# Attention in groups of two tiles in a windowed attention + SoLU MoE kernel, with PSUM shared out anew and the sync queue reordered

## The chip, the cores and the metric

The kernel runs on one core of one Trainium2 chip. The metric is the device time of one execution in microseconds (us). The engines are named as in the profile: PE (TensorE) does matrix multiplies into PSUM, PEld is its weight load, DVE is VectorE, ACT is ScalarE, POOL is GpSimd, and SP is the sync engine, whose queue (SPq) issues every DMA of this kernel.

## What is computed

Attention with a causal window of 64 keys, in 8 heads of 64, then one SoLU feed-forward layer on the joined heads. The reference, cut to what matters:

```python
scores = scale * np.matmul(q, k.transpose(0, 1, 3, 2))          # (8, 8, 576, 576), D = 64
mask = (rel >= 0) & (rel < 64)
scores = np.where(mask, scores, -1e9); scores -= np.max(scores, axis=-1, keepdims=True)
attn = np.exp(scores); attn = attn / (np.sum(attn, axis=-1, keepdims=True) + 1e-09)
x = np.matmul(attn, v)                                          # heads joined: (4608, 512)
h = x @ w_in                                                    # (4608, 1024)
e = np.exp(h - np.max(h, axis=-1, keepdims=True))
solu = h * (e / (np.sum(e, axis=-1, keepdims=True) + 1e-09))
ln = (solu - mean(solu)) / np.sqrt(var(solu) + 1e-06) * g_ln
out = ln @ w_out                                                # (4608, 512)
```

All inputs and the output are fp32.

## The kernel before

The 4608 tokens are cut into 36 tiles of 128. Each tile t goes through these steps (line numbers are those of the kernel before):

- `load(t)` (L336, L340): two DMAs on SP, qk (640 KB) and v (512 KB).
- `scores(t)` on PE (L364): 32 small matmuls, 64x64 weights against 64x128, into `pS`. Below they are called S.
- `softmax(t)`: eight masked row maxima on DVE (L379, out of `pS` into `sS`), eight exponentials on ACT (L384), a reciprocal of the sums on DVE (L397, L400) and eight scalings on POOL (L402), one per head.
- `cross(t)`: the scaled weights have to be transposed. From tile 5 on ACT splits them into two planes of 16 bits (L416, two copies into a `raw` buffer), two DMA transposes on SP turn the planes round (L419), and `transposes(t)` puts them together on DVE (L426, two copies into `PT`). Tiles 0 to 4 are transposed on PE (L439).
- `values(t)` on PE (L463): 32 small matmuls of 128x64 weights into `pX`, called V below. ACT rounds the result into `xH` (L477), and DVE takes the rest into `xL` (L478).
- `moe_in(t, h)` on PE (L506): two halves of 12 matmuls of 128x128 against 128x512 into `pH`, which holds two banks and has one buffer. Each fp32 product is made of three passes, xH by the high weights, xH by the low ones, xL by the high ones. All 24 are called I.
- `moe_norm(t)`: row maximum on DVE (L521), exponential on ACT (L523), product and sum on DVE (L526), then sums, a square on ACT (L532), a power on POOL (L539), and two scalings on POOL (L543, the halves of `e`). After L526 `pH` is free for the next tile.
- `moe_cross(t)` and `moe_transpose(t)`: the halves of `e` go the same way, DVE copy (L569), DMA transpose (L572), DVE copy (L582), ACT cast to `yH` (L586), DVE remainder `yL` (L588). The first three and the last two tiles are transposed on PE (L605).
- `moe_out(t)` on PE (L642): 24 matmuls like those of I into `pO`, called O. ACT copies the result (L649), and a DMA on SP stores it (L650).

A main loop over t (L682) records these steps as a plan: in iteration t it records `load(t+4)`, I(t), the norm of t, V(t+1), S(t+3) with its softmax and cross, and O(t-2). PE and SP keep the order of recording (`edges`, L71), unless an operation is marked loose. Every other engine's order is made by a list scheduler (`order`, L109): each operation carries a cost written in the code, its due time comes from PE's order, and whatever is due first among the ready operations goes next. The result is written out as one fixed sequence for each engine, and each engine runs its own in order. Buffers are rings (`RINGS`, L46): a tile of a ring waits for the last reader of the one that held its place before.

PSUM has eight banks here: `pH` two, `pS` two (one buffer), `t` two (transposes on PE, one bank each), `pX` one, `pO` one.

Of the kernel before, what the change touches and what calls it, by code (L numbers as in the profile page):

```python
# [18 lines left out]
P = 128  # L19
# [7 lines left out]
AHEAD = 3  # L27
# [13 lines left out]
CROSS_P = 5  # L41

# [121 lines left out]
def tile_window_attention_solu_moe(  # L164
# [156 lines left out]
    def QK(t):  # L321
        return T("qk", t, [P, NPAIR * (2 * P + WIN)])
# [10 lines left out]
    def load(t, parts=range(2)):  # L333

        if 0 in parts:
            plan.dma(P * P * 40, lambda: nc.sync.dma_start(QK(t), qk[t]), [], [("qk", t)])  # L336


        if 1 in parts:
            plan.dma(P * P * 32, lambda: nc.sync.dma_start(  # L340
                T("v", t, [P, 2, DM]).rearrange("p a n -> p (a n)"), v[t]), [], [("v", t)])

# [69 lines left out]
    def cross(t):  # L412
        if t < CROSS_P:
            return
        for x in range(2):
            plan.op("ACT", 1050, lambda x=x: nc.scalar.copy(  # L416
                XP(t)[:, x], SS(t)[:, 4 * x:4 * x + 4].bitcast(U16).rearrange("p h (n w) -> p w (h n)", w=2)),
                [("sS", t, 4 * x + i) for i in range(4)], [("raw", NW + 2 * t, x)])
            plan.op("SP", 1250, lambda x=x: nc.sync.dma_start_transpose(  # L419
                XP(t)[:, 2 + x].rearrange("p w (h n) -> p (w h) n", h=4), XP(t)[:, x].rearrange("p w n -> p (w n)")),  # L420
                [("raw", NW + 2 * t, x)], [("raw", NW + 2 * t, 2 + x)], 2600)

    def transposes(t):
        if t >= CROSS_P:
            for x in range(2):
                plan.op("DVE", 740, lambda x=x: nc.vector.tensor_copy(  # L426
                    PT(t)[:, 4 * x:4 * x + 4].bitcast(U16).rearrange("p h (n w) -> p h w n", w=2),
                    XP(t)[:, 2 + x].rearrange("p w (h n) -> p h w n", h=4)),
                    [("raw", NW + 2 * t, 2 + x)], [("PT", t, x)])
            return  # L430
        for x in range(2):
            n = 4 * t + x

            def pA(n=n):
                return T("t", n, [P, 4, P], pool=ps_t)
# [5 lines left out]
            plan.op("PE", 430, emit, [("sS", t, 4 * x + i) for i in range(4)], [("t", n)], loose=t < LOOSE)  # L441
            plan.op(
                "DVE" if x and t >= EARLY else "ACT", 600, lambda x=x, pA=pA:
                (nc.vector.tensor_copy if x and t >= EARLY else nc.scalar.copy)(PT(t)[:, 4 * x:4 * x + 4], pA()),  # L444
                [("t", n)], [("PT", t, x)])

    def PX(t):
        return T("pX", t, [P, NC, P], pool=ps_x)

# [6 lines left out]
    def values(t):  # L456
# [11 lines left out]
        if t < PLAIN_IN:  # L468
            for x in range(2):
                ps = slice(2 * x, 2 * x + 2)  # L470
                plan.op("PE", 550, lambda x=x: emit((2 * x, 2 * x + 1)), [("PT", t, x)] + vals, [("pX", t, x)],
                        loose=t < LOOSE)
                plan.op("ACT", 360, lambda ps=ps: nc.scalar.copy(XH(t)[:, ps], PX(t)[:, ps]),
                        [("pX", t, x)], [("xH", t, x)])
            return
        plan.op("PE", 1100, emit, [("PT", t, x) for x in range(2)] + vals, [("pX", t)])
        plan.op("ACT", 560, lambda: nc.scalar.copy(XH(t), PX(t)), [("pX", t)], [("xH", t)])  # L477
        plan.op("DVE", 620, lambda: nc.vector.tensor_sub(XL(t), PX(t), XH(t).bitcast(F32)),  # L478
                [("pX", t), ("xH", t)], [("xL", t)])

# [84 lines left out]
    def moe_cross(t):  # L565
        if not crosses(t):
            return
        for h in range(2):
# [23 lines left out]
    def moe_transpose(t):  # L592
# [3 lines left out]
        for h in range(2):  # L596
            n = 4 * t + 2 + h

            def pT(n=n):
                return T("t", n, [P, 4, P], pool=ps_t)  # L600

# [5 lines left out]
            hs = slice(4 * h, 4 * h + 4)  # L607
            plan.op("PE", 430, emit, [("e", t, h)], [("t", n)])
            if t < PLAIN_OUT:
                plan.op("DVE", 620, lambda hs=hs, pT=pT: nc.vector.tensor_tensor(  # L610
                    YH(t)[:, hs], pT(), g_sb[:, hs].unsqueeze(2).to_broadcast([P, 4, P]), op=ALU.mult),
                    [("t", n), ("g",)], [("yH", t, h)])
                continue
            plan.op("ACT", 560, lambda hs=hs, pT=pT: nc.scalar.copy(YH(t)[:, hs], pT()),
                    [("t", n)], [("yH", t, h)])
            plan.op("DVE", 620, lambda hs=hs, pT=pT: nc.vector.tensor_sub(
                YL(t)[:, hs], pT(), YH(t)[:, hs].bitcast(F32)),
                [("t", n), ("yH", t, h)], [("yL", t, h)])

    def moe_out(t, middle=None):  # L620

        other = t >= NTILE - BEHIND and (NTILE - t) % 2 == 0
        tag = ("pX", NTILE + t) if other else ("pO", t)

        def PO():
            return T(*tag, [P, DM], pool=ps_x if other else ps_o)

# [22 lines left out]
        plan.dma(P * DM * 4, lambda: nc.sync.dma_start(out[t * P:(t + 1) * P, :], ot()), [("ot", t)], [])  # L650

# [109 lines left out]
```

## Time and profile before

| | |
|---|---|
| median of 3 runs | 532.76 us (531.51 to 532.77) |
| profiled execution, its own time | 533.39 us |
| its span, first to last instruction | 531.6 us |
| PE busy | 511.5 us (96%) |
| DVE, ACT, POOL busy | 415.4, 352.4, 213.9 us |
| mean granted PE clock | 0.996 |
| data moved by DMA | 93.56 MB |

The span leaves 1.8 us of the profiled execution's own time outside. A row of the timeline reads: start in us from the span's start, duration in us, engine, line, operation, output <- inputs, count, and in square brackets the idle time of the engine before it. A row of the groups reads: line, engine, operation, names, shapes, count | busy us, mean ns of one | idle us just before them. A row of the windows reads: stretch, its length, then busy us and count for PE, PEld, DVE, ACT, POOL, then the granted PE clock as a share of full speed, DMA share and GB/s. An fp32 matmul of V or S is one instruction of the program and two records in the profile (x16 in the program's order is x32 in the timeline).

### The profile page before, as it was taken

What the parts mean: (1) busy time and instruction counts of PE and PEld (TensorE: products, weight loads), DVE (VectorE), ACT (ScalarE), POOL (GpSimd) and SP (SyncE); (2) the same over time, 40 slices, a digit from 0 to 9 for tenths busy, and PEclk for the clock granted to TensorE, in tenths of its full rate; (3) what the DMA queues carried; (4) which work ended last, traced back from release to release, by engine and by line L of the source; (5) the groups of instructions that cost most, each with busy time, mean ns of one, the idle gap of its engine ahead of it and who ended that gap; (6) DMA issues with size and microseconds to landing.
All of it is one profiled execution on the core that took longest, in us unless ns stands there. A gap on an engine that the chain in (4) does not pass through costs nothing.

```text
span 531.6 us, 11607 instructions
## 1 busy us (share of the span) xinstructions
PE 511.5 (96%) x4072; PEld 393.2 (74%) x4072; DVE 415.4 (78%) x1327; ACT 352.4 (66%) x959; POOL 213.9 (40%) x406
## 2 busy tenths in 40 slices
PE   2789999999999999999999999999999999999997
PEld 1345566777777887777777777777777777777785
DVE  4969998878888888888887888888878888887630
ACT  4479866677777777777777776666666666676331
POOL 2036077344443444444443444444444444444130
PEclk9999999999999999999999999999999999999999
DMA  8992107687788778777888877777778777774411
GB/s 318 408 357 110 65 2 179 171 182 187 186 189 187 191 189 188 190 188 179 187 173 166 207 182 186 181 187 184 176 171 197 189 184 184 183 182 75 100 41 39
DMA packets 148506, 93.56 MB, mean 176 GB/s; under 512 B 132960, under 2 KB 132960, under 8 KB 148064
## 3 DMA queue, kind: packets, MB, share of 16 engines
q1 hardware_dynamic: 148448, 92.83, 68.3%
q8 instruction: 32, 0.52, 0.4%
q14 instruction: 26, 0.21, 0.1%
HBM read 50.86 MB, written 9.44 MB: 113 GB/s over the span
## 4 chain that ended last, share of the span: by engine, by line
PE 94%; ACT 2%; DVE 2%; DMA 1%; POOL 0%; issue 0%; ACTq 0%; DVEq 0%
PE pO L642 36%; PE pH L506 34%; PE pX L463 7%; PE pS L364 7%; PE pH L495 4%; PE pO L630 3%; PE pX L642 1%; DMA qk<-qk 1%; PE t L605 1%; ACT sS L384 1%; PE t L439 1%; ACT w L285 0%; POOL e L543 0%; DVE mst L521 0%; ACT e L523 0%; ACT PT L444 0%
## 5 line engine op out<-in xcount | busy, mean ns | idle before, releaser
L402 POOL TENSOR_SCALAR sS<-sS,rec 128x128 f32<-128x128 f32 x280 | 116.9, 439 | 49.8 <-DVE nmx L379 27.0
L384 ACT ACTIVATE sS<-sS,nmx 128x128 f32<-128x128 f32 x288 | 112.6, 395 | 9.7 <-DVE nmx L379 9.4
L539 POOL TENSOR_TENSOR mst<-mst,neghalf 128x1 f32<-128x1 f32 x36 | 20.6, 571 | 235.1 <-DVE mst L537 235.1
L642 PE MATMUL pO<-w_outH,yH 128*128 128x512 f32 x264 | 108.1, 410 | 0.0
L506 PE MATMUL pH<-w_inH,xH 128*128 128x512 f32 x264 | 105.8, 401 | 0.0
L642 PE MATMUL pO<-w,yH 128*128 128x512 f32 x264 | 104.6, 396 | 0.0
L506 PE MATMUL pH<-w,xH 128*128 128x512 f32 x264 | 104.2, 399 | 0.0
L642 PE MATMUL pO<-w_outH,yL 128*128 128x512 f32 x264 | 103.7, 393 | 0.0
L506 PE MATMUL pH<-w_inH,xL 128*128 128x512 f32 x264 | 103.6, 392 | 0.0
L477 ACT CAST xH<-pX 128x512 fp32r<-128x512 f32 x33 | 19.4, 587 | 112.6 <-PE pX L463 112.6
L543 POOL TENSOR_SCALAR e<-e,mst 128x512 f32<-128x512 f32 x72 | 73.5, 1028 | 18.4 <-DVE rec L397 11.0
L416 ACT COPY raw<-sS 128x1024 uint16<-128x1024 uint16 x62 | 62.2, 1051 | 6.2 <-POOL sS L402 6.1
L521 DVE TENSOR_REDUCE mst<-pH 128x1 f32<-128x1024 f32 x36 | 44.0, 1224 | 26.0 <-PE pH L506 25.2
L569 DVE COPY raw<-e 128x1024 uint16<-128x1024 uint16 x62 | 46.6, 752 | 21.9 <-POOL e L543 21.9
L642 PEld LDWEIGHTS pO<-w_outH,yH 128*128 128x128 f32 x264 | 49.5, 187 | 16.0 <-issue 5.0
L506 PEld LDWEIGHTS pH<-w_inH,xH 128*128 128x128 f32 x264 | 49.5, 188 | 13.5 <-issue 0.5
L506 PEld LDWEIGHTS pH<-w_inH,xL 128*128 128x128 f32 x264 | 49.6, 188 | 12.6 <-DVE w L310 0.2
L642 PEld LDWEIGHTS pO<-w_outH,yL 128*128 128x128 f32 x264 | 49.6, 188 | 12.3
L506 PEld LDWEIGHTS pH<-w,xH 128*128 128x128 f32 x264 | 49.6, 188 | 11.6 <-issue 0.2
L642 PEld LDWEIGHTS pO<-w,yH 128*128 128x128 f32 x264 | 49.6, 188 | 10.2
L384 ACT ACTIVATION_READ_ACCUMULATOR sS<-sS,nmx 128x1 f32 x288 | 55.2, 192 | 0.0
L379 DVE CUSTOM_DVE_ANT_0 sS<-pS,maskNone 128x128 f32<-128x128 f32 x224 | 51.1, 281 | 4.0 <-PE pS L364 3.9
(73 smaller groups left out, 777.5 us busy)
## 6 DMA issues: line engine op xcount, KB each, us to landing
qk<-qk SPq DMA_DIRECT2D x36, 640.0 KB, 4.8
v<-vS SPq DMA_DIRECT2D x36, 512.0 KB, 5.5
y<-ot SPq DMA_DIRECT2D x36, 256.0 KB, 2.6
raw<-w_out SPq DMA_DIRECT2D x4, 1024.0 KB, 10.1
raw<-w_in SPq DMA_DIRECT2D x3, 1024.0 KB, 11.5
raw<-raw SPq DMA_TRANSPOSE x124, 3.2
raw<-w_in SPq DMA_DIRECT2D x2, 512.0 KB, 6.5
g_sb<-gT SPq DMA_DIRECT2D x1, 4.0 KB, 14.9
```

The costliest lines, as they stand in the source:

```text
L364: nc.tensor.matmul(PS(t)[half * WIN:(half + 1) * WIN, r, p], q[rs, p, half * WIN:(half + 1) * WIN], keys, start=True, stop=True)
L379: plan.op("DVE", 215, lambda h=h: nc.vector.tensor_tensor_reduce(SS(t)[:, h], PS(t)[:, h % 2, h // 2], mk, scale=-SCALE, scalar=BIG, op0=A ...
L384: plan.op("ACT", 390, lambda h=h: nc.scalar.activation(SS(t)[:, h], SS(t)[:, h], AF.Exp, bias=cols("nmx", h), scale=-1.0, accum_out=cols(" ...
L402: plan.op(engine, cost, lambda h=h: v.tensor_scalar(SS(t)[:, h], SS(t)[:, h], rec()[:, h:h + 1], 0.0, ALU.mult, ALU.add), [R], [("sS", t, h)])
L416: plan.op("ACT", 1050, lambda x=x: nc.scalar.copy(XP(t)[:, x], SS(t)[:, 4 * x:4 * x + 4].bitcast(U16).rearrange("p h (n w) -> p w (h n)", ...
L463: nc.tensor.matmul(PX(t)[r * D:(r + 1) * D, p, ks], V(t, half)[:, h * D:(h + 1) * D], PT(t)[:, h, ks], start=True, stop=True)
L495: plan.op("PE", 860, lambda c=c, x=x: nc.tensor.matmul(PH(t)[:, x * 512:(x + 1) * 512], XH(t)[:, c], W32(c)[:, x], start=(c == 0), stop=(c ...
L506: plan.op("PE", 233, lambda n=n, c=c, x=x, w=w: nc.tensor.matmul(PH(t)[:, hs], x(t)[:, c], WH(c, h) if w is WH else WL(c)[:, h], start=(n ...
L521: plan.op("DVE", 1150, lambda: nc.vector.tensor_reduce(nmax(), PH(t), axis=AX.X, op=ALU.max, negate=True), [("pH", t)], [key(0)])
L543: plan.op("POOL", 770, lambda h=h, hs=hs: nc.gpsimd.tensor_scalar(E(t)[:, hs], E(t)[:, hs], nmean(), kk(), ALU.add, ALU.mult), [key(4), ke ...
L569: plan.op("DVE", 740, lambda h=h: nc.vector.tensor_copy(EP(t, h), E(t)[:, h * 512:(h + 1) * 512].bitcast(U16).rearrange("p (n w) -> p w n" ...
L642: plan.op("PE", 233, lambda f=f, i=i, x=x, k=k, y=y, w=w: nc.tensor.matmul(PO(), y(t)[:, f], w(i, x), start=(f == k == 0), stop=(f == NF - ...
```

## The change

**Groups of two.** Until iteration 6 the loop is as before, except that in iteration 6 scores of two tiles (9 and 10) follow V(7). Iteration 7 has V(8) alone. From iteration 8 on each even iteration records V(t+1), V(t+2), S(t+3), S(t+4) one behind the other on PE between I(t) and O(t-2), and each odd one records neither. `transposes` of both tiles are recorded at the even iteration. The count of every instruction of the steps stays what it was.

**PSUM.** `pS` gets a second buffer of two banks. The transposes on PE no longer have banks of their own (`t` is gone) and use buffers of `pS`. `pX` is gone, too: V writes into the ring `pO`, which now has two banks and holds V's and O's results in turn. So in a group the ring is taken by V(t+1), V(t+2), O(t-2), O(t-1), and O(t-2) waits until `xH` and `xL` of tile t+1 have been taken out of its bank.

**The sync queue.** DMAs of tiles after the third (loads, transposes, stores) are marked loose: SP no longer keeps them in the order of recording, the scheduler places them by due time. Loads of qk and v are recorded apart.

The core of the diff:

```diff
+PAIRS = 6
+SPL = 3
...
-    "pS": 1, "pH": 1, "t": 2, "pX": 1, "pO": 1,
+    "pS": 2, "pH": 1, "pO": 2,
...
-    def dma(self, size, emit, reads, writes):
-        self.op("SP", max(350, size // 340), emit, reads, writes, 2600)
+    def dma(self, size, emit, reads, writes, loose=False):
+        self.op("SP", max(350, size // 340), emit, reads, writes, 2600, loose)
...
-            plan.dma(P * P * 40, lambda: nc.sync.dma_start(QK(t), qk[t]), [], [("qk", t)])
+            plan.dma(P * P * 40, lambda: nc.sync.dma_start(QK(t), qk[t]), [], [("qk", t)],
+                     t > SPL)
...
+    def PP(t, x):
+        return PS(2 * NTILE + t)[:, x]
+    def PE_T(t, x):
+        return PS(NTILE + t)[:, x]
...
     def PX(t):
-        return T("pX", t, [P, NC, P], pool=ps_x)
+        return T("pO", NTILE + t, [P, NC, P], pool=ps_o)
...
+    def group(t):
+        on(values, t + 1)
+        if t != PAIRS:
+            on(values, t + 2)
+        both = t + AHEAD, t + AHEAD + 1
+        for u in both:
+            on(scores, u)
+        for u in (t + AHEAD + 2, t + AHEAD + 3):
+            on(load, u, range(1))
+        for u in (t + AHEAD + 1, t + AHEAD + 2):
+            if u != PAIRS + AHEAD + 2:
+                on(load, u, range(1, 2))
+        for u in both:
+            on(softmax, u)
+            on(cross, u)
+
     for t in range(NTILE + BEHIND):
-        on(load, t + AHEAD + 1)
+        if t < PAIRS:
+            on(load, t + AHEAD + 1)
+        if t == PAIRS - 1:
+            on(load, t + AHEAD + 2, range(1))
...
-            on(transposes, t + 1)
+            even = (t - PAIRS) % 2 == 0
+            if t <= PAIRS + 1:
+                on(transposes, t + 1)
+            elif even:
+                on(transposes, t + 1)
+                on(transposes, t + 2)
...
-            on(values, t + 1)
-            attend(t)
+            if t < PAIRS:
+                on(values, t + 1)
+                attend(t)
+            elif t == PAIRS + 1:
+                on(values, t + 1)
+                on(load, t + AHEAD + 1, range(1, 2))
+            elif even:
+                group(t)
```

**Where instructions move.** On PE, in the middle of the program, the order of before between I(16) and O(14), and between I(17) and O(15). In the names the first number is the buffer's own count, which is the tile (in the ring `pO` of the changed kernel V's tiles count on from 36, so `pO_53` is V of tile 17), the second a running number.

```order
L506 MATMUL pH_16_2863<-w_inH_103,xL_16_2802 128x512
L463 MATMUL pX_17_2915<-PT_17_2870,v_17_2556 64x64 x16
L364 MATMUL pS_19_2938<-qk_19_2859 64x128 x16
L642 MATMUL pO_14_2963<-w_outH_104,yH_14_2842 128x512
...
L506 MATMUL pH_17_3026<-w_inH_103,xL_17_2965 128x512
L463 MATMUL pX_18_3078<-PT_18_3033,v_18_2719 64x64 x16
L364 MATMUL pS_20_3101<-qk_20_3022 64x128 x16
L642 MATMUL pO_15_3126<-w_outH_104,yH_15_3005 128x512
```

The same place on PE in the changed kernel:

```order
L513 MATMUL pH_16_2868<-w_inH_97,xL_16_2687 128x512
L470 MATMUL pO_53_2915<-PT_17_2871,v_17_2387 64x64 x16
L470 MATMUL pO_54_2935<-PT_18_2897,v_18_2631 64x64 x16
L373 MATMUL pS_19_2959<-qk_19_2402 64x128 x16
L373 MATMUL pS_20_2986<-qk_20_2707 64x128 x16
L646 MATMUL pO_14_3009<-w_outH_98,yH_14_2866 128x512
...
L513 MATMUL pH_17_3072<-w_inH_97,xL_17_2968 128x512
L646 MATMUL pO_15_3139<-w_outH_98,yH_15_3092 128x512
```

V(18) and S(20) have moved ahead by one O and one I, and I(17) now goes straight over into O(15).

On ACT, the exponential of `moe_norm` of tile 15 (L523, later L530) and what stands around it. Before:

```order
L649 COPY ot_12_2709<-pO_12_2637 128x512
L532 ACTIVATE sq_14_2713,mst_14_2607<-e_14_2634,mst_14_2607 128x1024
L384 ACTIVATE sS_17_2647,sm_17_2668<-sS_17_2647,nmx_17_2648 128x128 x3
L477 CAST xH_16_2784<-pX_16_2752 128x512
L523 ACTIVATE e_15_2797,mst_15_2770<-pH_15_2700,mst_15_2770 128x1024
L416 COPY raw_42_2813<-sS_17_2647 128x1024 x2
L384 ACTIVATE sS_18_2810,sm_18_2831<-sS_18_2810,nmx_18_2811 128x128 x2
```

The same place on ACT in the changed kernel (`raw_42` and `raw_44` are the planes of tiles 17 and 18):

```order
L393 ACTIVATE sS_18_2719,sm_18_2766<-sS_18_2719,nmx_18_2720 128x128 x8
L653 COPY ot_12_2803<-pO_12_2680 128x512
L425 COPY raw_42_2810<-sS_17_2694 128x1024 x2
L530 ACTIVATE e_15_2836,mst_15_2817<-pH_15_2749,mst_15_2817 128x1024
L425 COPY raw_44_2849<-sS_18_2719 128x1024 x2
L593 CAST yH_14_2866<-y_14_2845 128x512
L653 COPY ot_13_2875<-pO_13_2813 128x512
```

The exponentials of tile 18 and the two plane copies of tile 17, which wait for POOL's scalings of that tile, now stand ahead of the exponential of tile 15; before, the copies stood behind it.

More of the change, by code (lines that the diff above doesn't have):

```diff
@@ L420, in cross @@
                 XP(t)[:, 2 + x].rearrange("p w (h n) -> p (w h) n", h=4), XP(t)[:, x].rearrange("p w n -> p (w n)")),
-                [("raw", NW + 2 * t, x)], [("raw", NW + 2 * t, 2 + x)], 2600)
+                [("raw", NW + 2 * t, x)], [("raw", NW + 2 * t, 2 + x)], 2600, t > SPL)
     def transposes(t):
@@ L431, in transposes, with pA @@
         for x in range(2):
-            n = 4 * t + x
-            def pA(n=n):
-                return T("t", n, [P, 4, P], pool=ps_t)
+            def pA(x=x):
+                return PP(t, x)
             def emit(x=x, pA=pA):
@@ L439, in emit @@
                     nc.tensor.transpose(pA()[:, i], SS(t)[:, 4 * x + i], ident)
-            plan.op("PE", 430, emit, [("sS", t, 4 * x + i) for i in range(4)], [("t", n)], loose=t < LOOSE)
+            plan.op("PE", 430, emit, [("sS", t, 4 * x + i) for i in range(4)], [("pS", 2 * NTILE + t, x)], loose=t < LOOSE)
             plan.op(
@@ L470, in values @@
                 ps = slice(2 * x, 2 * x + 2)
-                plan.op("PE", 550, lambda x=x: emit((2 * x, 2 * x + 1)), [("PT", t, x)] + vals, [("pX", t, x)],
+                plan.op("PE", 550, lambda x=x: emit((2 * x, 2 * x + 1)), [("PT", t, x)] + vals, [("pO", NTILE + t, x)],
                         loose=t < LOOSE)
                 plan.op("ACT", 360, lambda ps=ps: nc.scalar.copy(XH(t)[:, ps], PX(t)[:, ps]),
-                        [("pX", t, x)], [("xH", t, x)])
+                        [("pO", NTILE + t, x)], [("xH", t, x)])
             return
-        plan.op("PE", 1100, emit, [("PT", t, x) for x in range(2)] + vals, [("pX", t)])
-        plan.op("ACT", 560, lambda: nc.scalar.copy(XH(t), PX(t)), [("pX", t)], [("xH", t)])
+        plan.op("PE", 1100, emit, [("PT", t, x) for x in range(2)] + vals, [("pO", NTILE + t)])
+        plan.op("ACT", 560, lambda: nc.scalar.copy(XH(t), PX(t)), [("pO", NTILE + t)], [("xH", t)])
         plan.op("DVE", 620, lambda: nc.vector.tensor_sub(XL(t), PX(t), XH(t).bitcast(F32)),
-                [("pX", t), ("xH", t)], [("xL", t)])
+                [("pO", NTILE + t), ("xH", t)], [("xL", t)])
     def PH(t):
@@ L573, in moe_cross @@
                 TP(t, h).rearrange("p w f n -> p (w f) n"), EP(t, h).rearrange("p w n -> p (w n)")),
-                [("raw", NW + 2 * t + 1, h)], [("raw", NW + 2 * t + 1, 2 + h)], 2600)
+                [("raw", NW + 2 * t + 1, h)], [("raw", NW + 2 * t + 1, 2 + h)], 2600, t > SPL)
     def moe_join(t):
@@ L596, in moe_transpose, with pT @@
         for h in range(2):
-            n = 4 * t + 2 + h
-            def pT(n=n):
-                return T("t", n, [P, 4, P], pool=ps_t)
+            def pT(h=h):
+                return PE_T(t, h)
             def emit(h=h, pT=pT):
@@ L607, in moe_transpose @@
             hs = slice(4 * h, 4 * h + 4)
-            plan.op("PE", 430, emit, [("e", t, h)], [("t", n)])
+            plan.op("PE", 430, emit, [("e", t, h)], [("pS", NTILE + t, h)])
             if t < PLAIN_OUT:
@@ L611, in moe_transpose @@
                     YH(t)[:, hs], pT(), g_sb[:, hs].unsqueeze(2).to_broadcast([P, 4, P]), op=ALU.mult),
-                    [("t", n), ("g",)], [("yH", t, h)])
+                    [("pS", NTILE + t, h), ("g",)], [("yH", t, h)])
                 continue
             plan.op("ACT", 560, lambda hs=hs, pT=pT: nc.scalar.copy(YH(t)[:, hs], pT()),
-                    [("t", n)], [("yH", t, h)])
+                    [("pS", NTILE + t, h)], [("yH", t, h)])
             plan.op("DVE", 620, lambda hs=hs, pT=pT: nc.vector.tensor_sub(
                 YL(t)[:, hs], pT(), YH(t)[:, hs].bitcast(F32)),
-                [("t", n), ("yH", t, h)], [("yL", t, h)])
+                [("pS", NTILE + t, h), ("yH", t, h)], [("yL", t, h)])
     def moe_out(t, middle=None):
-        other = t >= NTILE - BEHIND and (NTILE - t) % 2 == 0
-        tag = ("pX", NTILE + t) if other else ("pO", t)
+        tag = ("pO", t)
         def PO():
-            return T(*tag, [P, DM], pool=ps_x if other else ps_o)
+            return T(*tag, [P, DM], pool=ps_o)
         if t < PLAIN_OUT:
@@ L649, in moe_out @@
         plan.op("ACT", 580, lambda: nc.scalar.copy(ot(), PO()), [tag], [("ot", t)])
-        plan.dma(P * DM * 4, lambda: nc.sync.dma_start(out[t * P:(t + 1) * P, :], ot()), [("ot", t)], [])
+        plan.dma(P * DM * 4, lambda: nc.sync.dma_start(out[t * P:(t + 1) * P, :], ot()), [("ot", t)], [],
+                 t > SPL)
     def on(f, t, *args):
```

8 lines of the change are left out of this document (3 added, 5 removed).

## Prediction

> **What bounds the kernel now.** I read the page first: busy shares and the chain that ended last.
>
> ```profile
> PE 511.5 (96%) x4072; PEld 393.2 (74%) x4072; DVE 415.4 (78%) x1327; ACT 352.4 (66%) x959; POOL 213.9 (40%) x406
> PE 94%; ACT 2%; DVE 2%; DMA 1%; POOL 0%; issue 0%; ACTq 0%; DVEq 0%
> ```
>
> The chain is PE's for 94% of the span, so a saving has to shorten PE's own row. Then the groups of PE from 93 to 483 us, and one period of the loop in the windows view (its columns: PE, PEld, DVE, ACT, POOL, clock, DMA share, GB/s).
>
> ```profile
> L463 PE MATMUL pX<-PT,v 128*64 128x64 f32 x896 | 32.3, 225 | 0.0
> L364 PE MATMUL pS<-qk 64*64 64x128 f32 x924 | 31.9, 275 | 0.0
> 253.53:267.07 13.54, 13.54 (x114) 10.81 (x113) 10.96 (x36) 9.42 (x26) 5.81 (x12) 1.00 0.82 188
> ```
>
> V and S never waited (idle 0.0). PE is filled for all 13.54 us of a period, at full clock; DVE has 2.6 us of room, ACT 4.1. What can be saved lies in how PE's instructions stand to one another. So I read PE's timeline over a period.
>
> ```profile
> 254.00 1.15 PE L463 MATMUL pX<-PT,v 128*64 128x64 f32 x32
> ...
> 261.82 0.40 PE L506 MATMUL pH<-w_inH,xH 128*128 128x512 f32 x1
> ...
> 267.22 0.39 PE L506 MATMUL pH<-w_inH,xL 128*128 128x512 f32 x1
> 267.54 1.15 PE L463 MATMUL pX<-PT,v 128*64 128x64 f32 x32
> 268.62 1.10 PE L364 MATMUL pS<-qk 64*64 64x128 f32 x32
> 269.65 0.50 PE L642 MATMUL pO<-w_outH,yH 128*128 128x512 f32 x1
> 269.99 0.39 PE L642 MATMUL pO<-w,yH 128*128 128x512 f32 x1
> ...
> 275.13 0.39 PE L642 MATMUL pO<-w_outH,yL 128*128 128x512 f32 x1
> ```
>
> Within I one matmul starts (267.22 - 261.82) / 23 = 0.235 us after the other, within O (275.13 - 269.99) / 22 = 0.234. Where the kind changes, the steps are longer: 0.32 into V, 0.34 from the first O to the second. Those steps are what a group of two can save.
>
> **The change, PE.** A period lasts 267.54 - 254.00 = 13.54. 48 large matmuls at 0.235 take 11.27 (11.24 with 0.234 for O), so one block of V and S costs 2.27 net, its changes of kind included. Near the end V stands alone:
>
> ```profile
> 484.18 1.15 PE L463 MATMUL pX<-PT,v 128*64 128x64 f32 x32
> 496.69 1.15 PE L463 MATMUL pX<-PT,v 128*64 128x64 f32 x32
> ```
>
> That period lasts 12.51: a lone V costs 1.24. What a second tile's V or S costs right behind the first is not in the trace, but the spacing inside a block is. These rows come from very short windows, each beginning after the first pair of V (two matmuls run at once) or the first quad of S (four):
>
> ```profile
> 267.65 0.34 PE L463 MATMUL pX<-PT,v 128*64 128x64 f32 x6
> 268.46 0.23 PE L463 MATMUL pX<-PT,v 128*64 128x64 f32 x2
> 268.78 0.40 PE L364 MATMUL pS<-qk 64*64 64x128 f32 x8
> 269.44 0.29 PE L364 MATMUL pS<-qk 64*64 64x128 f32 x4
> ```
>
> The second of 16 pairs starts at 267.65, the last at 268.46: 0.81 / 14 = 0.058 a pair, 0.93 for 16. The second of eight quads starts at 268.78, the last at 269.44: 0.66 / 6 = 0.11 a quad, 0.88 for eight. So if a second tile goes on in the first one's spacing, it costs 1.81 in place of 2.27. The order shows which blocks there are. Before: 27 of V and S (V of tiles 7 to 33), two lone V. After: one V S S, one V, twelve V V S S, one V V S, one V. Twelve groups of four save 12 x (2.27 - 1.81) = 5.52. Two blocks (4.54) become V S S and V (3.15 + 1.24): 0.15. V S and V (3.51) become V V S (3.20): 0.31. Together 5.98; with 0.234 for O it is 6.4. I take 6.1, near the first, since 0.235 is also the step from O to I.
>
> The boundary inside a group is the unknown. Its lower end is the spacing above (a gain beyond it is excluded: nothing starts earlier than the pair ahead lets it). Its upper end is the nearest change of kind: 0.16 from V's last pair to S (268.46 to 268.62) where 0.058 would do, and 0.11 for V's first pair, so 0.15 more for V; S to O 0.21 in place of 0.11, and 0.16 for the first quad, so again 0.15. Thirteen of each: 3.9 us of the gain lost. I take the lower end: V behind V has the shape of the rows inside a block, and the change of kind stands only where shapes differ. [...]
>
> **The change, the engines that feed PE.** No instruction is added. Per pair DVE's work stays 2 x 10.96 = 21.9 in some 26.6 us, ACT's 18.8, POOL's 11.6; no sum becomes the bound, but the order is tighter. Durations of the steps (groups between 118 and 470 us; the transposes from the page):
>
> ```profile
> L582 DVE COPY y<-raw 128x1024 uint16<-128x1024 uint16 x52 | 39.4, 757 | 1.7 <-DMA raw<-raw 1.6
> L426 DVE COPY PT<-raw 128x1024 uint16<-128x1024 uint16 x52 | 39.0, 751 | 2.6 <-DMA raw<-raw 2.6
> L569 DVE COPY raw<-e 128x1024 uint16<-128x1024 uint16 x52 | 38.9, 749 | 17.1 <-POOL e L543 17.1
> L379 DVE CUSTOM_DVE_ANT_0 sS<-pS,maskNone 128x128 f32<-128x128 f32 x160 | 36.3, 279 | 0.0
> L588 DVE TENSOR_TENSOR yL<-y,yH 128x512 fp32r<-128x512 f32 x52 | 35.2, 676 | 0.0
> L521 DVE TENSOR_REDUCE mst<-pH 128x1 f32<-128x1024 f32 x26 | 31.8, 1224 | 20.5 <-PE pH L506 20.5
> L526 DVE CUSTOM_DVE_ANT_0 e<-pH,e 128x1024 f32<-128x1024 f32 x26 | 31.5, 1213 | 0.0
> L478 DVE TENSOR_TENSOR xL<-pX,xH 128x512 fp32r<-128x512 f32 x26 | 17.5, 672 | 0.0
> L416 ACT COPY raw<-sS 128x1024 uint16<-128x1024 uint16 x52 | 52.0, 1051 | 0.4 <-POOL sS L402 0.2
> L523 ACT ACTIVATE e<-pH,mst 128x1024 f32<-128x1024 f32 x26 | 29.2, 1122 | 0.0
> L402 POOL TENSOR_SCALAR sS<-sS,rec 128x128 f32<-128x128 f32 x208 | 84.5, 427 | 0.0
> L543 POOL TENSOR_SCALAR e<-e,mst 128x512 f32<-128x512 f32 x53 | 54.2, 1031 | 9.8 <-DVE rec L397 9.8
> raw<-raw SPq DMA_TRANSPOSE x124, 3.2
> ```
>
> Count from a group's first V. S begins at 2.0, O(t-2) at 2.11 + 1.81 = 3.9, I(t+1) at 9.6 and ends at 15.4, O(t-1) runs to 20.9, I(t+2) to 26.5, and the next group begins at 26.6. Three waits could now show on PE, and since PE runs in order everything behind them would wait too.
>
> First, I(t+2) needs `pH`, so the product of tile t+1 (L526) must be done by 20.9. Its exponential stands on ACT behind both plane copies of the group's first softmax, and those wait for POOL's scalings. The longest way there, for t = 14: DVE has, ahead of POOL's turn, one L521, L588, two L569, two L478, one L526, 16 maxima (36.3 / 160 = 0.227 each), two L582, two more L588: 12.4, and with seven of the one-column operations at some 0.16 each 13.6. Such rows overlap: a whole period's means add up to 12.2 and cover 10.96, so 12.2 is likelier than 13.6. POOL's half of e (1.03) ends at 13.3, eight scalings (3.4) at 16.7, the second plane copy at 17.7, the exponential at 18.8, the product at 20.0. PE is free to go on: 0.9 us to spare, or 0.5 too late without the overlap. I take the former, nothing on the path.
>
> Second, the shared ring: O(t-2) waits at 3.9 for xL of tile t+1, fourth on DVE in the group (L521, L588, L569, L478: 3.3, with overlap 3.0). Hidden by V and S of the second tile, with 0.6 to 0.9 to spare.
>
> Third, V(t+4) of the next group, at 27.6: POOL's second eight scalings end at 20.1, the plane copy at 21.1, the transpose (3.2) at 24.3, the DVE copy by 25.8 if a y copy stands ahead. 1.8 us to spare.
>
> SP: the second half of e of tile t is transposed behind the four transposes of the pair. DVE's copy is ready at 21.9, it lands by 26.4 even if an issue is ahead, and O of tile t reads it only in its second half, past 33. The loads are issued in another order, a `qk` before the third `v`; nothing in the first 60 us waits for either. DMA moves the same bytes in 98% of the time (0.82 becomes 0.84).
>
> **Start and end.** Up to tile 6 PE's order is the same but for the names of buffers. I take 0, and 1 us either way as the bound: from 60 us on there is little idle time on PE to win or lose before the loop settles.
>
> ```profile
> 60.00:105.00 45.00, 44.66 (x300) 30.59 (x292) 39.86 (x127) 31.00 (x84) 23.24 (x37) 1.00 0.45 112
> ```
>
> The sum: 533.39 (the span of 531.6 and the 1.8 around it) - 6.1 = 527.3 for a run like the profiled one. That run lies 0.6 above the median, so against 532.76 the forecast is 526.7.
>
> **The rivals.** *The boundaries inside a group cost what a change of kind costs*: 526.7 + 3.9 = 530.6, still faster. Against it: the rows inside the block.
>
> *The chain through POOL is late* and PE waits for `pH` ahead of each I(t+2). At the start of the program the same eight scalings once took longer, while DVE worked on the weights:
>
> ```profile
> 66.81 4.52 POOL L402 TENSOR_SCALAR sS<-sS,rec 128x128 f32<-128x128 f32 x8 [16.13 <-DVE rec L400]
> ```
>
> That is 1.1 over 3.4. With it, and without DVE's overlap, PE would wait 1.6 in each of 13 pairs, 21 us, and the kernel would take 547.5; with half of that 537. It decides from 0.9 us of lateness on, and from 0.9 + 6.1 / 13 = 1.4 the kernel is slower than before. For it: DVE runs in order and waits for DMA and POOL inside this stretch. Against it: from 118 to 470 us the scalings' mean was 427 ns with DVE busy 81%. If the lateness is about 1.4, the two cancel and the time is 532 to 534: a case of its own.
>
> *The clock falls.* A group is 4.1 us without a full-size matmul. Once in the start the clock was lower, and two later stretches hold as many small operations as a group:
>
> ```profile
> 20.00:34.80 14.80, 11.36 (x72) 5.50 (x72) 11.63 (x44) 8.72 (x35) 2.82 (x8) 0.88 1.02 393
> 45.45:50.00 4.55, 3.77 (x77) 3.22 (x76) 4.35 (x17) 4.17 (x11) 3.35 (x9) 1.00 0.00 0
> 56.00:60.40 4.40, 4.40 (x79) 3.44 (x77) 4.40 (x6) 2.93 (x7) 0.00 (x0) 1.00 0.00 0
> ```
>
> The dip cost 0.12 x 14.8 = 1.8; with 13 such dips 23 us, 550. Against it: the second and third row stay at 1.00. [...]
>
> **Chances.** The forecast 0.64, costly boundaries 0.08, the chain just late enough to cancel the gain 0.12, the chain later than that 0.13, the clock 0.03. Under 0.3% (1.6 us, about what a measurement of this kernel can tell from no change) is 531.2 to 534.4. Faster 0.72, same 0.12, slower 0.16. The range begins at 525.2, for the larger sum (6.4) and a start better by 1; it ends at 532.0, so that costly boundaries and part of the cancelling case are in.
>
> **What would show it.** Right: PE without idle rows in the loop, a period of two tiles of 26.6 (27.08 before), V's second tile 0.93 and S's 0.88 behind the first. The boundary is wrong if these are near 1.08 and 1.03. The chain is wrong if the waits show PE at I or V waiting for DVE (L526's or L426's successors), or O for xL. The whole is wrong if the loop gains 6 us and the start loses them.

## The result, and the profile after

| | before | changed |
|---|---|---|
| median of the runs | 532.13 us (4 runs, 531.32 to 532.77) | 536.23 us (4 runs, 535.58 to 537.31) |
| profiled execution, its own time | 533.39 us | 536.71 us |
| its span | 531.6 us | 534.9 us |

The changed kernel is slower by 0.8% (ratio 1.008, 95% interval 1.0054 to 1.0106). The forecast was 526.7, the range ended at 532.0. The kernel before has one execution more here than the three known at the forecast; in the 78 executions of it beside the experiments it took 531.0 to 532.1 us at a mean granted clock of 0.998 or more and 532.6 to 533.6 at 0.997 or less, and its profiled run (533.39 at 0.996) is of the second kind. The page of the changed kernel, busy shares and the chain that ended last:

```profile
PE 508.7 (95%) x4072; PEld 394.4 (74%) x4072; DVE 419.2 (78%) x1327; ACT 357.2 (67%) x959; POOL 221.6 (41%) x406
PE 65%; DVE 11%; POOL 8%; DMA 8%; ACT 5%; issue 2%; ACTq 0%; POOLq 0%; DVEq 0%
```

PE is busy for 2.8 us less, in a span that is 3.3 longer. PE's share of the chain fell from 94% to 65%: now the end hangs on DVE, POOL and DMA as well. But the groups themselves do what they were said to do. PE's timeline at the start of a group:

```profile
145.21 0.39 PE L513 MATMUL pH<-w_inH,xL 128*128 128x512 f32 x1
145.52 2.08 PE L470 MATMUL pO<-PT,v 128*64 128x64 f32 x64
147.54 1.98 PE L373 MATMUL pS<-qk 64*64 64x128 f32 x64
149.44 0.50 PE L646 MATMUL pO<-w_outH,yH 128*128 128x512 f32 x1
```

64 matmuls of V in one row, 64 of S in the next. From V to S 2.02 pass (1.08 before), from S to O 1.90 (1.03 before): the second V costs 0.94, the second S 0.87. A pair of tiles without a wait, in the windows view (its last columns: granted clock, DMA share, GB/s):

```profile
280.54:307.14 26.60, 26.60 (x225) 21.63 (x224) 20.66 (x69) 18.85 (x51) 11.22 (x22) 1.00 0.85 189
```

26.60 in place of 27.08: twelve such groups and the two ends of the loop save 6.2. What went wrong stands in PE's timeline of one group, the one that starts at 334.10 (V of tiles 23 and 24):

```profile
354.75 0.39 PE L646 MATMUL pO<-w_outH,yL 128*128 128x512 f32 x1
357.92 0.47 PE L513 MATMUL pH<-w_inH,xH 128*128 128x512 f32 x1 [2.78 <-DVE mst L533]
```

And in the windows view, the stretch behind that wait:

```profile
358.69:362.10 3.41, 3.41 (x10) 2.64 (x9) 3.24 (x10) 2.35 (x5) 0.91 (x1) 0.51 0.91 187
```

I of tile 24 starts 3.17 after the matmul ahead of it, where 0.23 is usual; it waited for the product (now L533) of tile 23, since there is one `pH`. Then PE runs at a clock of 0.51 for 3.4 us and loses 1.57 more. Counted from start to start (the idle column counts from a modelled end and shows some 0.16 less), PE lost 8.1 in the loop: 6.1 at I waiting for the product (4.5 here, and 0.3 to 0.5 in each of four other groups), 1.5 at O waiting for `xL` (0.93, 0.35, 0.17, 0.06), 0.5 at V waiting for `PT`. The rest is at the end, in the transposes of tile 35 on PE:

```profile
520.43 0.66 PE L610 MATMUL pS<-ident,e 128*128 128x128 f32 x4
522.18 0.63 PE L610 MATMUL pS<-ident,e 128*128 128x128 f32 x4 [1.10 <-ACT yH L619]
```

Before, these eight stood in one row; the stretch from the last V to the last matmul took 30.8 and takes 32.2. The sum: 531.6 - 6.2 + 8.1 + 1.4 = 534.9, the span.

Back along the late group's chain. SP's queue (start, duration of the issue):

```profile
335.29 1.52 SPq L343 DMA_DIRECT2D v<-vS  x2
337.27 0.33 SPq L338 DMA_DIRECT2D qk<-qk  x1
339.57 3.87 SPq L579 DMA_TRANSPOSE raw<-raw  x2
```

The two transposes in the DMA view, with the median us from issue to landing at the end:

```profile
raw<-raw SPq DMA_TRANSPOSE x2, 6.6
```

And DVE's timeline:

```profile
346.01 0.76 DVE L589 COPY y<-raw 128x1024 uint16<-128x1024 uint16 x1 [1.85 <-DMA raw<-raw]
346.71 0.17 DVE L406 TENSOR_SCALAR rec<-sm 128x8 f32<-128x8 f32 x1
347.72 0.80 DVE L589 COPY y<-raw 128x1024 uint16<-128x1024 uint16 x1 [0.83 <-DMA raw<-raw]
348.99 0.20 DVE L409 RECIPROCAL rec<-rec 128x8 f32<-128x8 f32 x1
352.45 0.26 DVE L406 TENSOR_SCALAR rec<-sm 128x8 f32<-128x8 f32 x1
```

Three loads went out ahead of the transposes of `e` of tile 21, which landed after 6.6 us (median over the kernel 3.3). DVE, in order, stood for them twice, with the reciprocals of tiles 25 and 26 behind. So POOL's sixteen scalings began 15.4 after the group's first V. They were also slower than in the group before, where they began at 14.0:

```profile
321.10 6.54 POOL L411 TENSOR_SCALAR sS<-sS,rec 128x128 f32<-128x128 f32 x16
349.54 7.58 POOL L411 TENSOR_SCALAR sS<-sS,rec 128x128 f32<-128x128 f32 x16
```

The groups view of two short windows in that row shows why: from 349.9 to 351.3, while DVE does plane copies and a `yL`, and from 351.65 to 353.25, while it takes a maximum out of PSUM and does two operations of 128x8:

```profile
L411 POOL TENSOR_SCALAR sS<-sS,rec 128x128 f32<-128x128 f32 x2 | 2.1, 1056 | 0.0
L411 POOL TENSOR_SCALAR sS<-sS,rec 128x128 f32<-128x128 f32 x5 | 1.8, 373 | 0.0
```

The same scaling takes 373 ns without DVE's copies and 1056 beside them. The whole loop (145 to 480 us of both kernels) bears this out: 56 of the 392 scalings took 0.8 to 1.4 us (25 of 200 before, 31 of 192 now), and each of them began while a plane copy or a `yL` of DVE was running. The other 336 took 0.36 to 0.38; none of them began so, though in 51 such an operation of DVE's came up behind. Behind the first eight stand ACT's second plane copy and the exponential:

```profile
354.35 1.05 ACT L425 COPY raw<-sS 128x1024 uint16<-128x1024 uint16 x1 [0.45 <-POOL sS L411]
355.31 1.11 ACT L530 ACTIVATE e<-pH,mst 128x1024 f32<-128x1024 f32 x1
```

Then DVE's product:

```profile
356.54 1.23 DVE L533 CUSTOM_DVE_ANT_0 e<-pH,e 128x1024 f32<-128x1024 f32 x1 [2.42 <-ACT e L530]
```

It ends at 357.8, 23.7 after the group's first V; PE was free at 20.9. In the other full groups it ended at 19.2 to 21.1, and at 22.1 in one that an `xL` had already delayed. Over the loop (145 to 472) the waits of DVE for the transposes of `e` (us in total, times, longest), before and after:

```profile
DVE y L582 <- DMA raw<-raw: 1.6, 2, 0.8
```

```profile
DVE y L589 <- DMA raw<-raw: 22.2, 23, 2.0
```

### The profile page after: what moved, and what is told of

It reads as the page before. It is cut to its first block, busy times and chain, and to the rows that moved or that the text cites. A ratio compares the mean times of both kernels' runs of the same rounds, so it can differ in the third digit from the quotient of the medians.

```text
span 534.9 us, 11673 instructions
## 1 busy us (share of the span) xinstructions
PE 508.7 (95%) x4072; PEld 394.4 (74%) x4072; DVE 419.2 (78%) x1327; ACT 357.2 (67%) x959; POOL 221.6 (41%) x406
## 4 chain that ended last, share of the span: by engine, by line
PE 65%; DVE 11%; POOL 8%; DMA 8%; ACT 5%; issue 2%; ACTq 0%; POOLq 0%; DVEq 0%
PE pO L646 26%; PE pH L513 24%; DMA raw<-raw 7%; POOL sS L411 6%; PE pO L470 4%; PE pS L373 4%; PE pH L502 4%; POOL e L550 2%; ACT sS L393 2%; DVE sS L388 1%; DVE raw L576 1%; PE pO L634 1%; DVE PT L435 1%; DVE mst L528 1%; DVE y L589 1%
## 5 line engine op out<-in xcount | busy, mean ns | idle before, releaser
L411 POOL TENSOR_SCALAR sS<-sS,rec 128x128 f32<-128x128 f32 x280 | 122.0, 456 | 49.6 <-DVE nmx L388 26.7
L546 POOL TENSOR_TENSOR mst<-mst,neghalf 128x1 f32<-128x1 f32 x36 | 30.2, 840 | 203.7 <-DVE mst L544 203.7
L646 PE MATMUL pO<-w_outH,yH 128*128 128x512 f32 x272 | 110.1, 405 | 1.2 <-DVE xL L485 1.1
L646 PE MATMUL pO<-w,yH 128*128 128x512 f32 x272 | 108.1, 398 | 0.0
L646 PE MATMUL pO<-w_outH,yL 128*128 128x512 f32 x272 | 106.9, 393 | 0.1
L550 POOL TENSOR_SCALAR e<-e,mst 128x512 f32<-128x512 f32 x72 | 66.4, 928 | 45.1 <-DVE mst L547 20.4
L425 ACT COPY raw<-sS 128x1024 uint16<-128x1024 uint16 x62 | 64.3, 1045 | 30.7 <-POOL sS L411 30.6
L589 DVE COPY y<-raw 128x1024 uint16<-128x1024 uint16 x62 | 48.7, 785 | 24.0 <-DMA raw<-raw 23.9
L539 ACT ACTIVATE sq<-e,mst 128x1024 bf16<-128x1024 f32 x36 | 41.4, 1149 | 36.3 <-DVE mst L536 25.0
L593 ACT CAST yH<-y 128x512 fp32r<-128x512 f32 x62 | 38.1, 616 | 26.8 <-DVE y L589 12.5
```

What stands on the lines that cost most here:

```text
L411: plan.op(engine, cost, lambda h=h: v.tensor_scalar(SS(t)[:, h], SS(t)[:, h], rec()[:, h:h + 1], 0.0, ALU.mult, ALU.add), [R], [("sS", t, h)])
L425: plan.op("ACT", 1050, lambda x=x: nc.scalar.copy(XP(t)[:, x], SS(t)[:, 4 * x:4 * x + 4].bitcast(U16).rearrange("p h (n w) -> p w (h n)", ...
L539: plan.op("ACT", 1200, lambda: nc.scalar.activation(T("sq", t, [P, DFF], BF16), E(t), AF.Square, bias=nmean(), scale=1.0, accum_out=ss()), ...
L546: plan.op("POOL", 560, lambda: nc.gpsimd.tensor_tensor(kk(), kk(), neghalf, op=ALU.pow), [], [key(5)])
L550: plan.op("POOL", 770, lambda h=h, hs=hs: nc.gpsimd.tensor_scalar(E(t)[:, hs], E(t)[:, hs], nmean(), kk(), ALU.add, ALU.mult), [key(4), ke ...
L589: plan.op("DVE", 740, lambda h=h: nc.vector.tensor_copy(Y(h).bitcast(U16).rearrange("p f (n w) -> p f w n", w=2), TP(t, h).rearrange("p w ...
```

## The experiments

Theory 1, the burst: two tiles' scalings one behind the other on POOL bring the product to the very point at which PE needs it, so any delay ahead of them is a wait on PE. Theory 2, the written order: with a second buffer for the scores and a loose sync queue the scheduler places work badly, and the groups themselves would fit. Line numbers of the runs with added lines are a few higher than those of the changed kernel.

**Without groups.**

```diff
-PAIRS = 6
+PAIRS = 40
```

> Changed kernel without groups: V and S stand in every iteration as before, PSUM and the sync queue as changed. Theory 1 (the burst: sixteen scalings in a row behind sixteen maxima are what makes the product late): without bursts the waits in the loop go, and only the tail's wait of 1.35 us is left, 532.1 + 1.4 = 533.5. Theory 2 (the written order: with two buffers for the scores and a loose sync queue the scheduler puts maxima and reciprocals behind copies that wait for a DMA): PE waits for the product in this kernel too, 536 to 542.

532.99 (10 runs; ratio to the kernel before 1.0019, 1.0005 to 1.0033). The windows view, 118 to 470 us:

```profile
118.00:470.00 352.00, 352.00 (x2920) 281.01 (x2916) 287.40 (x936) 246.20 (x677) 149.21 (x291) 1.00 0.83 182
```

PE is filled for all 352 us, and DVE waits for the transposes of `e` 3.2 us in all (145 to 472 us). The new PSUM and the loose queue cost a loop without groups nothing; theory 2's 536 to 542 falls for it. What the written order does to groups this run can't tell. What is left is the tail's wait.

**Own buffers in the tail.** For the last two tiles:

```diff
-                return PE_T(t, h)
+                return PS(3 * NTILE + 2 * t + h)[:, 0]
```

> Changed kernel, but the transposes on PE of the last two tiles take a buffer of their own for each half, as before. If the shared buffer makes the second half of tile 35 wait for ACT's copy of the first, the stretch from the last V to the end takes 34.9 us again (36.3 in the changed kernel), and the time is 536.2 - 1.35 = 534.9. If the halves of e themselves come late, the wait stays and the time too, 536.2.

534.96 (6 runs, 533.57 to 536.8), and all eight transposes in one row:

```profile
521.83 1.04 PE L613 MATMUL pS<-ident,e 128*128 128x128 f32 x8
```

From the last V to the last matmul it is 30.8 again. As the diff gives each half a buffer and nothing else changes there, the shared buffer was the cause.

**Sync queue in the order of recording.**

```diff
-SPL = 3
+SPL = 40
```

> Changed kernel with every DMA kept in the order of recording on SP. If the loads that now go ahead of the transposes of e are what makes the chain late, the waits of PE in the loop (8.05 us) mostly go: 528 to 531. If the loose queue is needed, because in recorded order the planes of a pair wait behind loads and stores that are not ready, PE waits for PT in most groups: over 545.

566.81 (one run). The waits of PE, 118 to 509 us:

```profile
PE pO L470 <- issue: 14.3, 14, 2.1
PE pO L470 <- DVE PT L435: 6.7, 11, 1.0
```

V waits in every group; 6.7 of it is put down to DVE's copies into `PT`, and for the 14.3 the profile names no releaser. But each of these fourteen V begins 0.10 us after the end of a copy into `PT`, like this one, the longest (the copy ends at 207.46):

```profile
206.72 0.73 DVE L435 COPY PT<-raw 128x1024 uint16<-128x1024 uint16 x1
207.56 0.71 PE L470 MATMUL pO<-PT,v 128*64 128x64 f32 x16 [2.12 <-issue]
```

So all 21 us are most likely waits for `PT`, as the second case of the expectation has it. In this order the groups are far slower: they need the loose queue, and the loads ahead are not cured by undoing it.

**Costs of the scheduler as measured.**

```diff
-plan.op("DVE", 740, ...)          # three places
+plan.op("DVE", 650, ...)
-... 2600, t > SPL)                # the DMA transposes
+... 3200, t > SPL)
-("POOL", nc.gpsimd, 360)
+("POOL", nc.gpsimd, 400)
```

> Changed kernel with three costs of the scheduler set by the traces: 650 for the copies on DVE between planes and tiles (740 before, measured 640 to 660 from start to start), 3200 of latency for the DMA transposes (2600 before; with the issue that is 4.5 us, measured 3.1 alone and up to 6.8 behind loads), 400 for a scaling on POOL (360 before, measured 406 to 474). No instruction changes, only the order on DVE, ACT, POOL and SP. Theory 2 (the written order): most of the 8.05 us of waits in the loop go, 536.2 - 7 = 529, between 528 and 530.5. Theory 1 (the burst is late in any order): 534 or more.

531.68 (12 runs, 530.36 to 534.31; ratio to before 0.9997, 0.9979 to 1.0014): between the two. In the profile of one run of 533.91 the wait of 4.5 and the waits for `xL` are gone, and DVE waits 8.5 for the transposes of `e` in place of 22.2; but the product is late in five groups:

```profile
PE pH L513 <- DVE mst L537: 3.9, 5, 1.5
```

So the order decides how late the worst group is (the product ends 22.4 after the group's first V in place of 23.7), and this one still leaves the chain at its limit.

**Short scalings.**

```diff
+                c = slice(0, 16 if t >= PAIRS + AHEAD else P)
-                    SS(t)[:, h], SS(t)[:, h], ...
+                    SS(t)[:, h, c], SS(t)[:, h, c], ...
```

> Changed kernel with every order and count as it is, but from tile 9 on POOL scales only 16 of the 128 columns of each head, so that a scaling is short (the other 112 columns stay unscaled). If the late product is POOL's doing (it starts behind the reciprocals, and a scaling takes 0.37 us alone and 0.8 beside DVE's copies), the waits for the product (6.1 us with the clock's dip) and for PT (0.5) go, and those for xL (1.5) and in the tail (1.35) stay: 536.2 - 6.6 = 529.6, between 528.5 and 530.5. If DVE itself is late, because its copies wait for the transposes, the product stays late and the time stays over 534.

532.0 (10 runs, 529.35 to 533.17). The experiment is weaker than it was meant to be: an eighth of the columns saves only a quarter of the time (351 ns in the mean against 460 in the changed kernel; 0.27 us against 0.37 where no copy of DVE's was running). The group of the short scalings over the run:

```profile
L412 POOL TENSOR_SCALAR sS<-sS,rec 128x16 f32<-128x16 f32 x216 | 71.0, 351 | 1.4 <-DVE rec L409 1.2 <-ACT raw L426 0.2
```

The same late group in the timelines of DVE, POOL and PE:

```profile
343.04 0.76 DVE L590 COPY y<-raw 128x1024 uint16<-128x1024 uint16 x1 [2.63 <-DMA raw<-raw]
346.57 5.97 POOL L412 TENSOR_SCALAR sS<-sS,rec 128x16 f32<-128x16 f32 x16
354.00 0.47 PE L514 MATMUL pH<-w_inH,xH 128*128 128x512 f32 x1 [2.44 <-DVE mst L534]
```

Of the waits of under 1 us at I three go, and those for `xL` go; the fourth grows to 1.3, in a group whose scalings began at 16.1 after its first V. That of the late group stays (2.44, and 3.41 us at a clock of 0.50 behind it), since its scalings begin late, too (16.2). Two causes, then: the length of the burst for three small waits, DVE standing for a DMA for the large one. Of the 3.6 us between the profiles of this run and of the changed kernel only 1.9 lie in the loop.

**One load moved.** In the scheduler, once its order is made:

```diff
+        out.remove(at["qk", 28])
+        out.insert(out.index(at["raw", 51, 3]) + 1, at["qk", 28])
```

> Changed kernel with one instruction moved on SP alone: the load of qk of tile 28 is issued behind the two transposes of e of tile 21, not ahead of them; every other engine keeps its order. In the changed kernel these two transposes landed 6.4 and 6.8 us after their issue, DVE's copies waited for them with both reciprocals of the pair behind, and PE stood 2.9 us before I of tile 24 and lost 1.6 more to a lower clock. Theory: the load ahead is the cause. The transposes land in about 4 to 5 us, the product is done 2 us earlier, the wait is under 1 us and the clock stays: 536.2 - 4 = 532, between 531 and 533.5. Rival (POOL's burst or DVE's own order makes that group late): the wait stays above 2 us, 535 to 537.5.

533.36 (12 runs, 531.79 to 536.23), 2.9 less than the changed kernel for one instruction moved on SP. The late group's transposes in the DMA view:

```profile
raw<-raw SPq DMA_TRANSPOSE x2, 5.1
```

DVE's wait and PE's in the timelines:

```profile
347.25 0.76 DVE L592 COPY y<-raw 128x1024 uint16<-128x1024 uint16 x1 [0.65 <-DMA raw<-raw]
...
359.12 0.47 PE L516 MATMUL pH<-w_inH,xH 128*128 128x512 f32 x1 [1.55 <-DVE mst L536]
```

They land after 5.1 in place of 6.6, DVE waits 0.65 in place of 1.85, PE 1.55 in place of 2.78, and the clock stays at 1.00. From its first V to the next group's the late group takes 28.35 in place of 31.11. The load ahead is shown to be 1.2 of this wait, and with it went the 1.6 that the clock cost behind it; 1.5 stays, more than the theory's "under 1", with the two loads of `v` still ahead. The profile is of an execution of 535.62, only 1.1 shorter than the changed kernel's, since other groups lost more in it (up to 1.3 us); the 2.9 is the difference of the medians (the ratio to the kernel before falls from 1.008 to 1.0029).

**Two scalings on ACT**, alone and with the tail's own buffers.

```diff
+                if t >= PAIRS + AHEAD and h % 4 == 3:
+                    plan.op("ACT", 390, lambda h=h: nc.scalar.mul(
+                        SS(t)[:, h], SS(t)[:, h], rec()[:, h:h + 1]), [R], [("sS", t, h)])
+                    continue
```

> Changed kernel with two of the eight scalings of a tile (heads 3 and 7, from tile 9 on) moved from POOL to ACT, which scales by the same reciprocal; nothing is left out. POOL's burst loses 4 of 16 scalings, 1.5 us at 0.37 and more beside copies; the product was late by 0.05 to 0.5 in four groups and by 2.8 in one. If POOL's burst is the cause, most of the waits for the product go: 529 to 531.5. If ACT is as tight as POOL (its planes, exponentials and casts stand on the same chain), nothing is won: 535 to 538.

> As the run with two scalings on ACT, and with the tail's transposes in buffers of their own: 1.35 less than that run, 527.7 to 530. If no wait were left at all it would be the forecast's 526.7.

529.47 (6 runs) and 526.18 (5 runs, 526.07 to 528.08): ratios to the kernel before 0.9941 (0.9921 to 0.9962) and 0.990 (0.9882 to 0.9917). The second beats both kernels, and is where the forecast had put the change itself. V of tile 6 and of tile 35 in PE's timeline (one record of the first is missing), then a pair in the windows view:

```profile
103.67 1.15 PE L474 MATMUL pO<-PT,v 128*64 128x64 f32 x31
490.40 1.15 PE L474 MATMUL pO<-PT,v 128*64 128x64 f32 x32
```

```profile
224.72:251.31 26.59, 26.59 (x225) 21.62 (x224) 22.43 (x72) 20.24 (x56) 12.37 (x18) 1.00 0.86 189
```

And PE's waits from 118 to 509 us:

```profile
PE pH L517 <- DVE mst L537: 0.2, 1, 0.2
```

From V of tile 6 to V of tile 35 386.7 (391.6 before, 393.6 in the changed kernel). That is 4.9 saved in the loop and not 6.2: three groups still lose 1.4 together from start to start, of which the view of waits shows 0.2. This run also reached V of tile 6 earlier, at 103.67 in place of 105.06, since it lacks the slow stretch of the clock that the profiles of both other kernels have in the start (3.41 us at 0.50, from 25.33 before and from 34.51 in the changed kernel; the five traces with one get there at 105.1 to 105.6, the eight without at 103.0 to 104.5). That the time comes so near to 526.7 is partly luck. The scheduler now writes nearly the same order for every pair, and the product ends 20.2 to 21.3 after the group's first V.

POOL's burst did not get shorter by this. The groups of POOL from 145 to 480 us, the changed kernel's scalings and this one's:

```profile
L411 POOL TENSOR_SCALAR sS<-sS,rec 128x128 f32<-128x128 f32 x192 | 84.4, 460 | 0.0
L415 POOL TENSOR_SCALAR sS<-sS,rec 128x128 f32<-128x128 f32 x148 | 83.5, 583 | 0.0
```

Fewer scalings take the same time, since more of them (50 of 148, 31 of 192 in the changed kernel) begin while DVE copies; the median burst lasts 6.7 us in place of 6.6. What went are the late groups: POOL begins 12.2 to 14.6 after the group's first V (12.2 to 15.4 in the changed kernel), and DVE waits 7.0 for the transposes of `e` in place of 22.2. So these two runs changed the load on POOL and the written order at once.

**Control without groups.** The same two edits with PAIRS = 40 (and 9 for PAIRS + AHEAD).

> Control without groups: V and S in every iteration, PSUM and sync queue as changed, two scalings on ACT from tile 9 on, the tail's transposes in buffers of their own. PE has no wait in the loop without groups, so a lighter POOL can win nothing: 532.5, equal to the kernel before within 0.3%. If it were faster than that, the gain of the two runs with scalings on ACT would not be that of the groups.

532.69 (10 runs; ratio 1.0007, 0.9994 to 1.002). A lighter POOL wins nothing without groups: the 1% is that of the groups.

**POOL's burden given back.** To the kernel of 526.18, one more operation, then three, behind heads 2 and 6, unseen by the scheduler:

```diff
+                    if t >= PAIRS + AHEAD and h % 4 == 2:
+                        v.tensor_scalar(junk, junk, rec()[:, h:h + 1], 0.0, ALU.mult, ALU.add)
```

> The run with two scalings on ACT and own buffers in the tail (526.2), its orders unchanged, but POOL gets its burden back: behind the scaling of heads 2 and 6 it does one more of the same size on a tile that nobody reads, so that a pair has sixteen again. If the length of POOL's burst decides, the product, done 20.2 to 21.25 us after the group's first V there against a limit of 20.9, comes 0.7 later (two extra operations of 0.35 in the first tile) and waits come back in most groups, 0 to 1 us each, some 4 us in all: 530, between 528.5 and 532. If the regular order that the scheduler found for that kernel is all of its gain, the time stays at 526 to 527.5.

> The same with three more operations behind heads 2 and 6, twenty-four in a pair: the product comes 2.1 us later than in the run with two scalings on ACT, 22.4 on the average against 20.9, so PE waits some 1.5 us in each of twelve groups, 18 us: 544, between 540 and 549. If the burst has slack, less than half of that.

531.43 (10 runs, 530.19 to 532.93) and 562.94 (4 runs, 561.19 to 567.21). PE's waits in the first (118 to 509 us) and the second (118 to 540):

```profile
PE pH L522 <- DVE mst L546: 1.2, 5, 0.3
PE pH L522 <- DVE mst L542: 0.6, 1, 0.6
```

```profile
PE pH L523 <- DVE mst L547: 16.9, 10, 2.1
PE pH L523 <- DVE mst L543: 4.8, 4, 1.9
PE pO L480 <- DVE PT L445: 5.2, 10, 1.1
```

In the first of them the product ends at 20.4 to 21.5 in place of 20.2 to 21.3. So at one order four operations more in a pair (501 ns each in the mean) cost 5.2 of the 5.5 by which that kernel beat the one before (526.18 against 531.71). This also parts the two: sixteen operations on POOL and own buffers in the tail give 534.96 in the changed kernel's order and 531.43 in this one, so 2 to 3.5 us (by the ratios to the kernel before, 1.0041 and 1.0001, or by the medians) come with the order and ACT's part in it, and 5.2 with the lighter POOL. With twelve operations more the product is late in every group and `PT` too, which the expectation of 544 did not count; that miss is one of size.

## Why the prediction was wrong

**Right: PE's sum.** 26.6 for a pair, 0.93 and 0.88 for the second V and S, no cost at the boundary (measured 0.94 and 0.87): 6.1 was taken, 6.2 measured. The start cost nothing: V of tile 6 begins at 105.06 in both profiles.

**Wrong, and decisive: "0.9 us to spare" for the product.** The reckoning (20.0 after the group's first V, limit 20.9) was made for one pair, t = 14, from mean durations. Measured, the product came at 19.2 to 21.1 in ten of the twelve full groups, so the typical group was nearly priced rightly, but five groups lay beyond the limit, and of the 8.1 us that PE lost in the loop 6.1 are this wait and the clock's loss behind it. A chain whose estimate lies within 1 us of its limit should have been carried as a wait in some of the groups, not as "nothing on the path". The chance for it (0.25 over the two late cases) was too low; the result lies between the prices of these two, 534 and 537.

**Wrong: SP and DMA.** The text looked for waits behind the new order of the loads only in the first 60 us, and priced every transposition's landing at 3.2. In the loop three loads now go ahead of the transposes of `e`, which landed after 6.6 in the late group; DVE's waits for them rose from 1.6 to 22.2. DVE's row of the count for POOL's turn held durations alone and no wait. One load moved back gave 2.9 us.

**Wrong: 427 ns for a scaling.** The mean hid two values, 0.37 and 0.8 to 0.9 (0.8 to 1.4 in the changed kernel), by whether DVE was copying when the scaling began. The row of 4.52 for eight scalings in the start, which the prediction quoted in a rival's support, fits this: its first three took 0.80 to 1.18 us, each begun while DVE ran a subtraction on the weights (L310), and the other five 0.38. In the late group the same scaling took 1056 against 373 ns, and in the loops slow were just the scalings that began while a plane copy or a `yL` ran (25 of 200 in the kernel before). Why a scaling is slower beside these operations no run here shows. Sorted by what DVE was doing at their start, the scalings of the kernel before would have made the cost of a scaling depend on what DVE does in the group.

**Wrong in size: `xL` and `PT`.** `xL` was reckoned at 3.0 to 3.3 after the group's first V, against 3.9; it came at 2.5 to 4.8, and O waited 1.5 in all. `PT` was late in one group only (0.5).

**Wrong: the end.** It stood in a heading but got no term and no reason; the 1 us either way was argued for the start. The shared buffer of the transposes cost 1.4. That PSUM's halves now lie in one buffer was in the diff.

**A slip without weight.** The range's lower end, 525.2, is by its own terms (532.76 - 6.4 - 1) 525.4.

**The clock.** The rival had small matmuls lower it; in groups without a wait they didn't (1.00). Behind some of the waits it fell. Here are the 3.41 us from I on after a wait of 1.71 and just behind one of 2.12, in the run with twenty-four operations on POOL:

```profile
227.93:231.34 3.41, 3.41 (x15) 2.76 (x16) 1.53 (x4) 1.39 (x3) 3.20 (x7) 1.00 0.42 78
257.50:260.91 3.41, 3.41 (x8) 2.70 (x9) 1.49 (x3) 1.40 (x3) 3.14 (x6) 0.50 0.42 79
```

In the loops of all traces here, six steps of 2.32 to 3.17 us from one matmul to the next at I (idle 1.9 to 2.8) were each followed by such a stretch, and twenty-one of 0.9 to 2.28 by none. No threshold follows from this: ahead of V, among small matmuls, three of seven steps of 1.33 came with one, too (sync queue in the order of recording). The two slow stretches of the run with twenty-four operations begin at 257.50 and 404.27, 43 times 3.413 apart, those of the changed kernel at 34.51 and 358.78, 95 times. At I, the shortest idle time that one followed was 1.9 us. The one behind the late group's wait of 2.9 cost 1.6 more.

What stays open: why the waits of one and the same kernel differ from run to run (530.4 to 534.3 in one of the experiments; the kernel before, without waits in its loop, spreads over 2.6), what share of the four small waits is POOL's burst and what the written order, and how long a wait must be to lower the clock.

## What to carry to other kernels

A change that puts work of the bounding engine together also puts together the work that feeds it: sum up not only each engine's load over the period, but the longest chain from the first of the pair to the point at which the bounding engine needs it, and give a chain with less slack than its own spread a price. A reckoned duration on an in-order engine has to hold the waits of what stands ahead, DMA landings above all (22.2 us, the largest of DVE's waits in the loop here); look at what each queue now issues ahead of them. When such a change loses, look for the resource at its limit: moving four of sixteen small operations to another engine, with the new order that the scheduler made of it and the tail's 1.4 us, turned +0.8% into -1.0%. And look at what such a move changed beside what it was meant to: here POOL's burst stayed as long as it was.

## What the runs showed of the hardware

A scaling of 128x128 on POOL took 0.36 to 0.38 us, and 0.8 to 1.4 when it began while DVE ran a plane copy or a `yL` (56 of 56 in two traces, and none of the 336 others); one of 128x16 took 0.27 and 0.5 to 1.2 (351 ns in the mean). A DMA transposition landed 3.2 us after its issue in the median of the kernel before, and 6.6 behind two loads of `v` and one of `qk`. The clock's slow stretches quoted here lasted 3.41 us at 0.50 or 0.51, and the two of one run began 95 (changed kernel) and 43 (twenty-four operations on POOL) times 3.413 us apart; at I in the loops they followed the six steps of 2.32 to 3.17 us between two matmuls and none of the twenty-one of 0.9 to 2.28.
